# Value weights that arrive already transposed: eight transposing loads in place of TensorE's turns, with a rewritten TensorE order

## The chip, the core and the metric

The kernel runs on one core of a Trainium2 chip. The core has five engines with a queue of instructions each: TensorE (PE: matmuls, with its weight loads shown as PEld), VectorE (DVE), ScalarE (ACT), GpSimd (POOL) and SyncE (SP). SP computes nothing here; it issues nearly all DMAs. The engines meet only through semaphores. On-chip data lies in SBUF (128 partitions); TensorE writes its results to PSUM, eight banks of 128 x 512 floats, and DVE or ACT must copy ("evict") them to SBUF before a bank is free again. The metric is device time in microseconds (us), the median of several runs of the whole program.

## The reference, cut to what matters

Two layers are applied to 2048 tokens of width 448, and each layer is an attention with a carried memory followed by a gated MLP. Attention goes over 64 segments of 32 tokens; each segment sees 8 memory rows besides its own tokens, and its own output at these 8 rows is the next segment's memory, so the segments form a chain.

```python
for s in range(n_seg):                                  # 64 segments, in order
    h = concat([mem, x[s]])                             # 8 + 32 rows of width 448
    q, k, v = h @ Wq, h @ Wk, h @ Wv                    # 16 heads of 256
    p = softmax(mask(q @ k.T * scale))
    o = einsum('bhte,hed->btd', p @ v, Wo)
    mem = o[:, :8]; outs.append(o[:, 8:])
...
x = x + A(layernorm(x)); x = x + B(layernorm(x))        # B: relu(x Wg) * (x Wu) @ Wd
x = x + A(layernorm(x)); x = x + B(layernorm(x))        # the same weights again
```

## The kernel before, in words

**Folded weights.** The kernel multiplies the weights together once, at the start. For each head it forms A = Wq Wk^T (448 x 448) and B = Wv Wo (448 x 448), and afterwards works on A and B alone: scores are h A h^T, and the output is (p h) B. TensorE contracts over partitions, so the product Wv Wo over the 256 head columns needs Wv with these columns on partitions. In DRAM Wv has its 448 rows first. The turned form is `lhs[e, et, d] = Wv[d, 128 et + e]`.

**The start, in order.** `weights` loads Wq and Wk in four groups (`g`), turns them on TensorE, and multiplies them into A. Then it goes over eight pairs of heads (`p`, 512 columns of Wv each). In the kernel before, a pair has four loads on SP's queue: rows 64 to 447 of Wv (`load`), two pieces with rows 0 to 63 (one for each head), and 448 KB of Wo. `transposes` (line 842, its last turn line 843) then turns each head with seven 128 x 128 matmuls against an identity into one PSUM bank. Two copies by DVE or ACT (line 399 is the ACT form, line 402 the DVE form) bring it to the `WT` buffers in SBUF. `product` (line 860) makes six products of 128 rows and one of the 64-row tails for a pair, each into a PSUM bank that is then copied into `Bsb`, the SBUF home of B.

**Buffers.** `Bsb` is also the staging area of Wq and Wk (slots 0 to 11), so a value product can be stored there only when the staged Wq and Wk of that place have been turned. A pair's Wv goes to slot `12 + p % 5`, its Wo to slot `p % 5`: pairs 5, 6 and 7 take over the slots of pairs 0, 1 and 2. Slots 12 to 14 lie in `glu` (the later home of the MLP weights), 15 and 16 in the two `Ug` buffers; the Wo slots lie in `glu`, `YT` and `hG`. The identity, the mask, and zeroed buffers are made by `constants` at the very start, together with dummy matmuls on zeros (line 303) that keep TensorE busy while the first weights arrive.

**After the start.** `chain` is one step of the memory recurrence (71 steps, the second layer seven segments behind the first): its matmuls with A (line 1029), the softmax in `middle` (lines 1186 to 1275), the matmuls with B (line 1066). `tiles` adds the attention of whole tiles of 128 tokens (lines 1356 to 1431) and the MLP (lines 1453 and 1471). `norm` prepares a tile (its turn is line 1304). `glu_part` issues the loads of the MLP weights (line 947) as steps complete.

**What sets the order.** A planner (`_Sched`) places every operation with estimated costs and writes one instruction list for each engine with the semaphore waits. TensorE's list isn't chosen by it: `ORDER` is a written permutation of all TensorE operations, and each waits in that order until its inputs and its banks are ready. A late operation holds up everything behind it on TensorE. For the other engines the planner takes whichever ready operation has the best priority. `turn` in `schedule` reads `ORDER`; `alias` entries tell which buffers share a place; `room` makes an operation wait for what its destination's next writer would have to wait for. The planner charges a DMA its bytes at 300 bytes per ns (`DMA_RATE`) and SP 620 ns for each issue (`DMA_ISSUE`).

Of the kernel before, what the change touches and what calls it, by code (L numbers as in the profile page):

```python
# [12 lines left out]
D = 448  # L13
# [392 lines left out]
def bass_interleave_layers__memory_aug_recurrent_mem_tr__glu_gated_reglu__prompt_kernel(  # L406
# [22 lines left out]
    0, 4, 1, 6, 5, 7, 15, 16, 30, 11, 14, 10, 9, 13, 18, 17, 2, 8, 12, 24, 23, 19, 20, 22, 25, 21, 27, 29, 39, 28,  # L429
    3, 26, 40, 38, 41, 35, 33, 34, 31, 47, 46, 32, 48, 37, 36, 44, 42, 45, 43, 62, 49, 50, 51, 52, 60, 61, 63, 54, 59, 53,  # L430
    57, 55, 66, 68, 67, 69, 56, 58, 64, 70, 65, 74, 72, 73, 71, 82, 83, 85, 84, 79, 80, 75, 76, 78, 91, 77, 81, 90, 89, 87,
    86, 88, 92, 111, 121, 112, 103, 102, 120, 118, 115, 94, 106, 125, 122, 104, 123, 105, 113, 93, 108, 127, 114, 124, 126, 109, 167, 168, 119, 128,
    110, 101, 169, 170, 116, 157, 165, 171, 107, 138, 98, 117, 173, 95, 147, 96, 97, 148, 156, 100, 172, 99, 129, 130, 149, 139, 154, 133, 174, 150,
    132, 161, 160, 151, 131, 140, 142, 163, 145, 136, 158, 137, 155, 146, 164, 159, 152, 144, 141, 134, 162, 143, 153, 175, 135, 176, 227, 177, 178, 228,
    229, 179, 180, 230, 184, 185, 182, 183, 181, 187, 186, 188, 231, 189, 232, 233, 241, 190, 242, 191, 243, 192, 193, 194, 244, 195, 199, 197, 200, 198,
    196, 202, 201, 203, 204, 245, 246, 247, 205, 255, 206, 256, 207, 208, 257, 166, 209, 210, 258, 212, 214, 213, 215, 211, 234, 216, 218, 217, 259, 219,
    260, 261, 269, 270, 220, 235, 248, 221, 236, 271, 272, 273, 274, 275, 237, 222, 223, 249, 238, 239, 224, 225, 262, 250, 295, 296, 293, 294, 226, 251,
    276, 298, 297, 299, 263, 240, 252, 264, 265, 300, 253, 254, 277, 301, 266, 302, 278, 279, 303, 304, 267, 268, 280, 305, 281, 306, 282, 308, 310, 309,
    311, 307, 283, 358, 284, 313, 312, 314, 285, 315, 359, 286, 316, 317, 287, 318, 319, 320, 288, 321, 323, 324, 325, 326, 322, 327, 328, 329, 289, 330,
    290, 292, 331, 291, 332, 368, 333, 334, 335, 338, 336, 337, 367, 360, 339, 341, 342, 340, 377, 344, 361, 345, 343, 352, 369, 346, 353, 385, 354, 347,  # L440
    362, 376, 363, 348, 386, 349, 350, 364, 370, 378, 351, 371, 372, 406, 404, 405, 407, 355, 365, 418, 410, 408, 409, 420, 366, 411, 373, 379, 356, 419,
    374, 421, 412, 357, 380, 413, 387, 381, 414, 415, 416, 375, 388, 382, 383, 422, 417, 389, 390, 426, 427, 424, 425, 429, 384, 428, 430, 391, 431, 392,
    393, 432, 439, 438, 440, 486, 423, 433, 494, 434, 394, 441, 435, 436, 395, 396, 437, 442, 446, 444, 447, 445, 443, 449, 459, 448, 450, 460, 458, 451,
    399, 400, 461, 452, 398, 453, 495, 454, 455, 456, 397, 485, 457, 462, 401, 402, 467, 468, 465, 466, 487, 470, 464, 469, 471, 496, 480, 403, 479, 472,
    503, 463, 473, 504, 474, 512, 481, 488, 475, 476, 477, 489, 490, 513, 497, 482, 505, 491, 498, 478, 492, 531, 533, 534, 532, 499, 506, 514, 537, 545,
    536, 546, 535, 493, 538, 483, 500, 484, 508, 507, 539, 501, 540, 622, 541, 542, 543, 547, 502, 509, 515, 510, 548, 544, 517, 516, 551, 552, 553, 554,
    511, 555, 557, 556, 549, 518, 558, 519, 520, 559, 566, 621, 550, 613, 560, 530, 567, 565, 521, 561, 562, 563, 522, 523, 564, 568, 573, 574, 571, 572,
    576, 526, 575, 577, 586, 585, 569, 578, 524, 579, 570, 580, 525, 581, 582, 583, 587, 612, 527, 588, 584, 528, 529, 614, 630, 631, 589, 623, 591, 639,
    590, 615, 594, 595, 592, 593, 617, 616, 640, 597, 596, 598, 606, 618, 619, 599, 620, 607, 608, 641, 624, 632, 600, 649, 601, 650, 626, 625, 602, 603,
    604, 633, 627, 651, 635, 675, 634, 605, 628, 694, 695, 696, 697, 629, 642, 609, 698, 700, 699, 643, 644, 666, 667, 701, 636, 637, 610, 652, 709, 702,  # L450
    668, 703, 611, 685, 704, 705, 706, 710, 708, 638, 645, 711, 646, 707, 647, 716, 714, 717, 715, 654, 653, 676, 729, 648, 655, 669, 712, 720, 719, 730,
    718, 656, 677, 721, 684, 713, 722, 659, 723, 776, 671, 724, 725, 726, 661, 670, 658, 660, 728, 727, 662, 734, 735, 736, 737, 657, 731, 738, 740, 686,
    739, 678, 749, 672, 741, 748, 750, 663, 664, 732, 742, 665, 743, 733, 785, 679, 744, 745, 746, 784, 680, 775, 693, 747, 751, 754, 757, 758, 755, 756,
    673, 759, 760, 769, 761, 674, 762, 681, 687, 771, 752, 786, 777, 763, 770, 753, 688, 764, 682, 765, 766, 767, 802, 794, 803, 768, 689, 832, 833, 830,
    831, 772, 778, 683, 835, 836, 834, 845, 844, 846, 690, 804, 837, 691, 773, 692, 847, 838, 780, 774, 839, 793, 779, 840, 841, 842, 787, 781, 789, 788,
    921, 782, 843, 795, 848, 850, 852, 851, 853, 783, 854, 796, 866, 856, 855, 790, 857, 797, 798, 791, 805, 858, 792, 849, 859, 807, 799, 806, 860, 861,
    862, 800, 864, 801, 865, 808, 863, 812, 867, 872, 870, 873, 871, 809, 875, 876, 874, 884, 885, 810, 877, 868, 911, 912, 869, 878, 811, 920, 879, 815,
    880, 881, 882, 813, 814, 816, 883, 817, 818, 819, 886, 922, 820, 913, 938, 930, 824, 939, 887, 890, 914, 822, 929, 821, 915, 916, 823, 893, 894, 891,
    892, 888, 825, 897, 896, 895, 826, 905, 898, 923, 827, 940, 906, 828, 931, 899, 889, 924, 900, 975, 901, 902, 903, 949, 925, 974, 950, 907, 904, 917,
    932, 1004, 1002, 1003, 1005, 908, 918, 1007, 1006, 1008, 829, 919, 934, 933, 926, 927, 941, 1009, 928, 935, 1018, 1016, 976, 1010, 909, 951, 1011, 910, 983, 943,  # L460
    942, 1012, 1013, 1014, 984, 992, 1017, 952, 936, 1015, 1019, 985, 1022, 1024, 1025, 1023, 1020, 937, 1027, 1038, 1026, 1028, 1037, 944, 1036, 1029, 945, 946, 1030, 953,
    1021, 993, 1031, 1083, 1032, 1033, 1034, 947, 1039, 1084, 954, 958, 959, 961, 960, 977, 1035, 962, 1042, 1044, 1045, 1043, 955, 1058, 1046, 1047, 1040, 1048, 1057, 963,
    948, 1049, 964, 956, 1050, 1056, 965, 1051, 1041, 969, 967, 979, 1052, 1053, 1054, 966, 978, 968, 1055, 986, 1059, 957, 980, 1062, 1065, 1066, 1063, 1064, 1068, 1060,
    1078, 994, 1069, 1079, 1067, 1085, 1077, 970, 1070, 971, 1080, 972, 1071, 973, 1061, 1072, 1093, 988, 987, 1073, 1074, 1075, 1081, 995, 1092, 1082, 981, 1076, 982, 1138,
    1140, 1141, 1139, 997, 996, 989, 1144, 1143, 1001, 1142, 990, 1145, 1152, 991, 1153, 1154, 1086, 1094, 1146, 1102, 1147, 1111, 1148, 1149, 1150, 1101, 1087, 1110, 1088, 1151,
    1103, 1095, 1160, 1158, 1161, 1159, 1155, 998, 1162, 1174, 1164, 1163, 1172, 1089, 1165, 999, 1000, 1090, 1166, 1156, 1112, 1167, 1157, 1220, 1096, 1097, 1168, 1169, 1170, 1104,
    1091, 1173, 1098, 1099, 1171, 1175, 1105, 1106, 1178, 1179, 1180, 1181, 1100, 1176, 1183, 1182, 1113, 1192, 1184, 1193, 1194, 1107, 1185, 1108, 1115, 1114, 1177, 1186, 1109, 1187,
    1228, 1188, 1189, 1190, 1116, 1120, 1117, 1118, 1195, 1191, 1219, 1229, 1221, 1119, 1237, 1238, 1121, 1122, 1123, 1124, 1125, 1196, 1126, 1230, 1239, 1222, 1127, 1128, 1130, 1223,
    1246, 1247, 1131, 1224, 1258, 1198, 1231, 1225, 1248, 1226, 1199, 1201, 1202, 1200, 1197, 1129, 1232, 1132, 1257, 1233, 1133, 1205, 1204, 1203, 1214, 1240, 1134, 1206, 1135, 1227,
    1234, 1215, 1136, 1207, 1259, 1235, 1242, 1208, 1241, 1236, 1249, 1209, 1210, 1211, 1251, 1283, 1250, 1282, 1243, 1213, 1212, 1244, 1312, 1310, 1311, 1313, 1137, 1245, 1216, 1316,  # L470
    1314, 1315, 1325, 1324, 1284, 1260, 1317, 1252, 1253, 1318, 1254, 1217, 1319, 1291, 1301, 1218, 1292, 1326, 1255, 1320, 1321, 1322, 1261, 1266, 1262, 1267, 1269, 1327, 1323, 1293,
    1332, 1330, 1333, 1331, 1263, 1336, 1256, 1334, 1335, 1345, 1328, 1346, 1264, 1337, 1270, 1271, 1285, 1344, 1338, 1265, 1339, 1329, 1275, 1287, 1340, 1341, 1342, 1286, 1268, 1274,
# [1126 lines left out]
```

## Time and profile before

| what | value |
|---|---|
| median of 3 runs | 1540.95 us (1539.51 to 1541.03) |
| profiled execution: its own time | 1542.45 us |
| profiled execution: span from first to last instruction | 1540.7 us |
| mean granted TensorE clock | 0.998 of full speed |
| instructions | 85641 |
| ScalarE busy | 870.4 us (56%) |
| GpSimd busy | 61.7 us (4%) |
| bytes moved by DMA | 34.20 MB, mean 22 GB/s |
| TensorE turns Wq and Wk, makes A | 6.8 to 44.7 us |
| TensorE turns Wv, makes B | 44.7 to 77.1 us |

The page splits the span into 40 slices of 38.5 us; the start that the change touches is the first two of them. Busy time of TensorE is modelled as if each matmul occupied it from start to end, so that matmuls that overlap are counted once. A line of the groups gives the engine, the source line, the operands by the program's names, the number of instructions, the busy time, and the mean duration of one. An idle time is followed by an arrow and what ended it. In the list of windows, the number after each engine is its busy time in that stretch, and x is the count of instructions.

### The profile page before, as it was taken

To read this page: it belongs to the slowest core of one execution; us is meant where nothing else is said; L and a number is where in the kernel's file an instruction comes from. 1 tells how busy PE (TensorE), PEld (TensorE's weight loads), DVE (VectorE), ACT (ScalarE), POOL (GpSimd) and SP (SyncE) were. 2 spreads that over 40 slices of the span, in tenths; PEclk is the share of its full clock that TensorE was granted. 3 is DMA by queue.
4 is the path that set the end of the run, shared out by engine and by line. 5 is a ranking of instruction groups with operands and counts; after the bars stand their busy time and mean duration, and the time that the engine had idled before them with its cause. 6 is when DMAs were issued, how large, how long until landed. Compare 5 with 4: busy or idle time off the path is not lost.

```text
span 1540.7 us, 85641 instructions
## 1 busy us (share of the span) xinstructions
PE 1525.0 (99%) x38921; PEld 1116.2 (72%) x38921; DVE 1154.1 (75%) x3388; ACT 870.4 (56%) x2434; POOL 61.7 (4%) x254
## 2 busy tenths in 40 slices
PE   9989999999999999999999999999999999999999
PEld 7567767677768777777768776777768776677676
DVE  7736678877877778768876878687877778677675
ACT  6844556555665655555654556455655556455543
POOL 1000000000000000000000000000000000000000
PEclk9999999999999999999999999999999999999999
DMA  8531000000000000000000000000000000000000
GB/s 244 159 88 49 10 8 12 8 9 8 8 5 14 8 8 14 5 15 6 17 5 7 13 9 14 5 15 7 18 5 7 13 5 17 4 9 7 8 11 12
DMA packets 44410, 34.20 MB, mean 22 GB/s; under 512 B 14216, under 2 KB 43152, under 8 KB 44048
## 3 DMA queue, kind: packets, MB, share of 16 engines
q1 hardware_dynamic: 43728, 28.45, 6.8%
q8 instruction: 307, 5.03, 1.3%
q14 instruction: 55, 0.45, 0.1%
q10 hardware_dynamic: 320, 0.26, 0.1%
HBM read 21.35 MB, written 1.84 MB: 15 GB/s over the span
## 4 chain that ended last, share of the span: by engine, by line
PE 94%; DVE 2%; SPq 2%; DMA 1%; issue 1%; ACT 1%; ACTq 0%; DVEq 0%
PE psG L1356 16%; PE psG L1431 16%; PE psC L1066 11%; PE psG L1453 11%; PE psC L1029 9%; PE psG L1471 5%; PE psG L1029 3%; PE psG L1271 3%; PE psG L1384 2%; PE psC L1186 2%; PE psG L1066 2%; PE psG L860 2%; PE psG L1186 2%; SPq L807 1%; PE psC L1209 1%; PE psC L1271 1%
## 5 line engine op out<-in xcount | busy, mean ns | idle before, releaser
L1431 PE MATMUL psG<-Bsb,YT 128*128 128x448 bf16 x1344 | 291.8, 353 | 0.0
L399 ACT ACTIVATE Ug<-psG 64x128 bf16<-64x128 f32 (+2 forms) x437 | 154.4, 368 | 85.0 <-PE psG L1356 67.4
L1431 PEld LDWEIGHTS psG<-Bsb,YT 128*128 128x128 bf16 x1344 | 115.9, 97 | 92.9 <-issue 8.9
L1453 PE MATMUL psG<-G,glu 64*128 64x128 bf16 x5544 | 182.6, 216 | 0.2 <-ACT hG L1458 0.2
L1453 PEld LDWEIGHTS psG<-G,glu 64*128 64x128 bf16 x5544 | 169.6, 94 | 7.6 <-issue 5.2
L1066 PE MATMUL psC<-Bsb,YTm 128*32 128x448 bf16 (+2 forms) x3752 | 171.8, 336 | 0.2 <-ACT YTm L399 0.2
L1356 PE MATMUL psG<-HT,A 64*128 64x128 bf16 x3256 | 171.1, 216 | 0.2 <-ACT Bsb L399 0.2
L1029 PE MATMUL psG<-A,mT 64*32 64x448 bf16 x4004 | 165.4, 350 | 0.5 <-DVE mT L402 0.2
L1029 PE MATMUL psC<-A,mT 64*32 64x448 bf16 x3836 | 162.2, 350 | 2.3 <-issue 1.7
L1356 PE MATMUL psG<-HX,A 64*128 64x128 bf16 x2442 | 146.0, 216 | 0.0
L1066 PEld LDWEIGHTS psC<-Bsb,YTm 128*32 128x32 bf16 x3752 | 94.1, 98 | 57.5 <-DVE YTm L402 0.7
L1029 PEld LDWEIGHTS psC<-A,mT 64*32 64x32 bf16 x3836 | 81.8, 92 | 58.0 <-ACT mT L399 3.7
L402 DVE CAST YT<-psG 128x448 bf16<-128x448 f32 x164 | 99.2, 617 | 27.2 <-PE psG L1275 26.4
L1356 PEld LDWEIGHTS psG<-HT,A 64*128 64x128 bf16 x3256 | 113.4, 94 | 7.6 <-issue 4.0
L399 ACT ACTIVATE YT<-psG 128x448 bf16<-128x448 f32 x205 | 104.5, 542 | 24.0 <-PE psG L1275 21.7
L402 DVE CAST Ug<-psG 64x128 bf16<-64x128 f32 (+2 forms) x245 | 105.0, 437 | 17.3 <-PE psG L1356 13.5
L1458 ACT ACTIVATE hG<-psG 128x512 bf16<-128x512 f32 (+1 forms) x121 | 65.9, 545 | 88.4 <-PE psG L1453 81.8
L1083 DVE TENSOR_TENSOR Osum<-psC,Osum 32x448 f32<-32x448 f32 (+2 forms) x110 | 67.0, 609 | 55.1 <-ACT Osum L1081 52.6
L1471 PE MATMUL psG<-glu,hG 128*128 128x448 bf16 x448 | 100.9, 353 | 0.0
L1029 PEld LDWEIGHTS psG<-A,mT 64*32 64x32 bf16 x4004 | 84.6, 92 | 18.2 <-issue 3.1
L1356 PE MATMUL psG<-l,A 64*128 64x128 bf16 x2821 | 96.7, 216 | 0.0
L1356 PEld LDWEIGHTS psG<-HX,A 64*128 64x128 bf16 x2442 | 92.4, 94 | 0.0
(295 smaller groups left out, 3126.8 us busy)
## 6 DMA issues: line engine op xcount, KB each, us to landing
Bsb<-in_A_Wq_dram SPq DMA_DIRECT2D x6, 384.0 KB
Bsb<-in_A_Wk_dram SPq DMA_DIRECT2D x6, 384.0 KB
glu<-in_A_Wv_dram SPq DMA_DIRECT2D x6, 384.0 KB
Tsb<-Ohi SPq DMA_DIRECT2D x128, 7.0 KB
X<-in_A_x_dram SPq DMA_DIRECT2D x16, 112.0 KB
glu<-in_A_Wo_dram SPq DMA_DIRECT2D x4, 448.0 KB
out_dram<-X SPq DMA_DIRECT2D x16, 112.0 KB
glu<-in_B_W_gate_dram SPq DMA_DIRECT2D x7, 224.0 KB
```

Of the source, the lines that this page charges most:

```text
L399: return E.activation(out, i, ACT.Copy, scale=1.0 if scale is None else scale)
L402: return E.tensor_copy(out, i)
L1029: i = E.matmul(ub[v].ap()[32 * j:32 * j + 32, 0:D], lhsT=self.mT[rw, b, :], rhs=self.A[rw, b, a0:a0 + D], start=(b == 0), stop=(b == 6), t ...
L1066: x = E.matmul(bo.ap()[32 * j:32 * j + 32, 0:d1 - d0], lhsT=self.YTm[:, q, :], rhs=self.Bsb[:, chunks[q], d0:d1], start=(i == 0), stop=(i ...
L1083: s.add("dve", dv_cost(n), lambda E, e, j=j, a_=a_, part=part: E.tensor_tensor(a_, part(j), a_, ALU.add), r=[bo], w=w, part=(j, 0), **P)
L1186: i = E.matmul(view()[:, :, k, v], lhsT=self.Usb[:, o:o + 128], rhs=Sel[:, :].rearrange("p (c q) -> p c q", c=2), start=True, stop=True)
L1271: return E.matmul(ps[:, n * q:n * q + n], lhsT=HR[rows, KM + 128 * q:KM + 128 * q + 128], rhs=PT, start=True, stop=True, tile_position=(b, 0))
L1356: i = E.matmul(ub[v].ap()[:, 128 * n:128 * n + 128], lhsT=self.A[rw, b, a0:a0 + 128], rhs=HT[rw, b, :, 0:SEG] if b < 4 else HX[rw, b - 4, ...
L1431: i = E.matmul(bo.ap()[:, 0:D], lhsT=YT[:, c, :], rhs=self.Bsb[:, 14 * g + c, :], start=(g == 0 and c == 0), stop=(g == 3 and c == 13))
L1453: i_ = E.matmul(two[v].ap()[:, 128 * c:128 * c + 128], lhsT=self.Wgu[rw, b, f0:f0 + 128], rhs=G[rw, b, :], start=(b == 0), stop=(b == 6), ...
L1458: s.add("act", 169 + 0.84 * N, lambda E, e, dst=dst, z=two[0], N=N: E.activation(dst, z.ap()[:, 0:N], ACT.Relu), r=[two[0]], w=[("hG", i, ...
L1471: i_ = E.matmul(bk.ap()[:, 0:D], lhsT=hG[:, c, :], rhs=self.Wd[:, c, :], start=(c == 0), stop=(c == NFC - 1))
```

## The change

A pair's Wv no longer comes by three loads and two sets of turns. One DMA (`turn_dma`, issued by SP with the transposing flag) reads the 448 x 512 block of Wv and writes it turned, as `V[e, a, d]` with 128 partitions and four blocks of 448, into the first 1792 columns of the same slot `12 + p % 5`. `product` reads its stationary operand straight from that slot. The eight pairs lose 24 loads, 112 turning matmuls and 32 copies, and get 8 transposing loads. The planner charges such a load 150000 bytes more than it carries.

A slot is now read by the pair's products, not by its turns, so the load of pair 5 waits for the products of pair 0 (and 6 for 1, 7 for 2). `product` gets `room=w`: it may not be placed before the operations that still use the place in `Bsb` to which its result goes. TensorE has 2711 operations in place of 2727, and its whole written order is another one, from the first entry to the last; the numbering shifts by up to 16 because of the removed operations.

```diff
 ORDER = (
-    0, 4, 1, 6, 5, 7, 15, 16, 30, 11, 14, 10, 9, 13, 18, 17, 2, 8, 12, 24, 23, 19, 20, 22, 25, 21, 27, 29, 39, 28,
...
+    4, 7, 0, 5, 6, 15, 1, 16, 2, 3, 30, 17, 18, 8, 11, 10, 14, 13, 21, 24, 12, 20, 25, 9, 23, 22, 19, 26, 39, 27,
...
 )
...
+    def turn_dma(self, dst, src, nbytes, r=(), w=(), prio=None):
+        self.s.add("sp", 60, lambda E, e: E.dma_start(dst, src, transpose=True), r=r, w=w, dma=nbytes + self.TURN_EXTRA, prio=prio)
+
+    TURN_EXTRA = 150000
...
-            s.add("pe", mm_cost(D, D), fn, r=[k for q in terms for k in q[5]], w=[bk], alloc=[bk], mode=mode, prio=0)
+            s.add("pe", mm_cost(D, D), fn, r=[k for q in terms for k in q[5]], w=[bk], alloc=[bk], room=w, mode=mode, prio=0)
...
         for p in range(NPAIR):
             sv = 12 + p % 5
             so = p % 5
-            load(self.Wv_d, p, sv)
-            for hh in range(2):
-                c = 512 * p + 256 * hh
-                self.dma(self.Wst[sv][64 * hh:64 * hh + 64, 3, 0:256], self.Wv_d[0:64, c:c + 256], 32768, w=[("Wt", sv, hh)])
+            V = self.Wst[sv].rearrange("p a b -> p (a b)")[:, 0:4 * D].rearrange("p (a b) -> p a b", a=4)
+            self.turn_dma(V, self.Wv_d[:, 512 * p:512 * p + 512], 458752, w=[(z, sv) for z in ("Wst", "Wst3")])
             self.dma(self.Wos[so][:, :, :], self.Wo_d[:, 4 * p:4 * p + 4, :], 458752, w=[("Wos", so)])
-            tv = nw()
-            transposes([(sv, hh) for hh in range(2)], tv, True, self.Wst[sv][:, 3, 0:256], [("Wt", sv, hh) for hh in range(2)])
             tails = []
             for hh in range(2):
-                r = tkeys(tv + hh) + [("Wos", so)]
-                rhs = self.Wos[so][:, 2 * hh:2 * hh + 2, :]
+                r = [("Wst", sv), ("Wos", so)]
+                lhs, rhs = V[:, 2 * hh:2 * hh + 2, :], self.Wos[so][:, 2 * hh:2 * hh + 2, :]
                 for k in range(3):
-                    product(self.Bsb[:, b_idx(k, p, hh), :], [(self.WT[tv + hh], 64 + 128 * k, 128, rhs, 0, r)], [("B", p, hh, k)], 0)
-                tails.append((self.WT[tv + hh], 0, 64, rhs, 64 * hh, r))
+                    product(self.Bsb[:, b_idx(k, p, hh), :], [(lhs, 64 + 128 * k, 128, rhs, 0, r)], [("B", p, hh, k)], 0)
+                tails.append((lhs, 0, 64, rhs, 64 * hh, r))
             product(self.Bsb[:, b_tail(p), :], tails, [("B", p, hh, 3) for hh in range(2)], 3)
```

In the new order, two products of pair 0 stand among the last products of A, and the first product of pair 4 stands ahead of the first of pair 3.

## The prediction

> **What bounds the kernel now.** I read the page's busy shares first, then its 40 slices.
>
> ```profile
> PE 1525.0 (99%) x38921; PEld 1116.2 (72%) x38921; DVE 1154.1 (75%) x3388; ACT 870.4 (56%) x2434; POOL 61.7 (4%) x254
> ...
> PE   9989999999999999999999999999999999999999
> ...
> DMA  8531000000000000000000000000000000000000
> ```
>
> TensorE has work in 99% of the span, and DMAs matter only in the first slices. So what is taken from TensorE shortens the run only if TensorE is also unbroken where the change sits. The busy time by stage (boundaries where turns of Wv start and products of B end) shows that:
>
> ```profile
> 36.00:44.70 8.70, 8.70 (x114) 6.21 (x112) 7.36 (x18) 7.11 (x14) 0.00 (x0) 1.00 1.08 345
> 44.70:77.10 32.40, 31.92 (x378) 19.23 (x376) 23.18 (x55) 27.60 (x60) 1.05 (x2) 1.00 0.42 124
> 77.10:150.00 72.90, 67.78 (x1880) 49.25 (x1880) 37.07 (x111) 33.14 (x96) 2.96 (x12) 0.98 0.28 72
> 150.00:300.00 150.00, 147.46 (x4041) 108.28 (x4047) 114.49 (x344) 84.91 (x247) 6.39 (x28) 1.00 0.04 10
> 300.00:1450.00 1150.00, 1148.85 (x30080) 845.16 (x30065) 887.79 (x2633) 655.43 (x1872) 43.31 (x184) 1.00 0.04 10
> ```
>
> Columns: stretch, length, busy time of PE, PEld, DVE, ACT and POOL, granted clock, DMA share, GB/s. In the B stage TensorE lacks 0.48 us of 32.40, DVE and ACT have room, and DMAs are at 42%. From 300 to 1450 us TensorE lacks 1.15 us. A saving made in the B stage is therefore not swallowed later. The waits of TensorE from 12 to 77 us are one line, a Wv load; the timeline beside it shows what a turn costs:
>
> ```profile
> PE psG L842 <- DMA Ug<-in_A_Wv_dram: 0.5, 1, 0.5
> ```
>
> ```profile
> 46.15 0.50 PE L842 MATMUL psG<-ident,glu 128*128 128x128 bf16 x6
> 46.48 0.22 PE L843 MATMUL psG<-ident,glu 128*128 128x128 bf16 x1
> 46.54 0.50 PE L842 MATMUL psG<-ident,glu 128*128 128x128 bf16 x6
> 46.87 0.22 PE L843 MATMUL psG<-ident,glu 128*128 128x128 bf16 x1
> 46.93 0.50 PE L842 MATMUL psG<-ident,glu 128*128 128x128 bf16 x6
> ```
>
> The seven turns of a head start 0.39 us after those of the one before (46.15, 46.54, 46.93): they overlap, and 0.39 us is what a set takes from TensorE. Last, SP's issues, and how the DMAs do on small packets (answer for 200 to 400 us):
>
> ```profile
> L807 SPq DMA_DIRECT2D glu<-in_A_Wv_dram x18: 376/586/1205, 31.3 to 54.2; - x18
> L807 SPq DMA_DIRECT2D Ug<-in_A_Wv_dram x6: 497/552/1587, 39.0 to 43.6; - x6
> L807 SPq DMA_DIRECT2D glu<-in_A_Wo_dram x4: 368/486/594, 33.7 to 65.0; - x4
> ```
>
> ```profile
> q1 hardware_dynamic: 3309, 1.07, 2.4%
> ```
>
> The first Wv is issued at 31.3 us, right after the last piece of Wk.
>
> **The change part by part.** *Turns removed.* 16 sets x 0.39 = 6.24 us of TensorE, on the path, since nothing else holds TensorE in this stage. The wait of 0.48 us at 45.3 goes if the first loads are early. As a check I walked both written orders with durations from the timeline (0.39 a set of turns, 0.392 a product of A, 0.379 a product of B, 0.73 a part of the memory's first product, 0.25 a norm's turn, 0.3 others), set so that the third group's products end where the trace has them. The old walk ends B at 76.9 us (trace 77.1), the new one at 70.6.
>
> The Trainium skill, TensorE: Matmul & The Clock Gate, Part 4, gives 275 ns for a turn in a kernel and says that turns don't raise the clock. By it 112 turns would be an estimated 30.8 us. The trace disagrees: 0.39 / 7 = 56 ns each, at a granted clock of 1.00 from 36 to 44.7 us, and 6.24 stands.
>
> *Copies removed.* 16 wide and 16 narrow, 13.0 us of DVE and ACT together in the group rows (ACT 6.8, DVE 6.2). Off the path: 0. What remains is 56 copies of 0.54 to 0.62 us, some 16 us an engine, in a stage of 26 us.
>
> *24 loads removed, 8 added.* SP issues two DMAs for a pair instead of four, 0.59 us each: 9.4 us less on its queue. Behind Wv and Wo stand only the loads of x for tiles 2 and 3, the memory rows and tile 1's rows, which are used after 100 us. If a transposing issue took the longest that a row of SP shows (1.8 us, a load of rows by line 807), five pairs would take 12 us in place of 13.6. Cost 0.
>
> *Time of a transposing load, T.* The trace has none. Nearest row for the bytes: 35 to 45 us at 338 GB/s, which makes 458752 B 1.36 us. Nearest row for small packets: 2.4% x 16 x 200 us / 3309 = 23.2 ns each. A source row of 512 columns falls into four pieces of 256 B, since each block has 128 partitions: 1792 pieces on 16 engines, 2.6 us. At the far end, single elements of 2 B would make 333 us a load. I take 2.0, between the first two, because whole pieces of rows are read as in the plain loads; the planner's own charge, 608752 B at 300 per ns, is 2.03.
>
> When does T reach the path? In the new walk the pairs' first products stand at 39.2 (0), 46.2 (1), 48.5 (2), 52.6 (4), 53.3 (3), 57.7 (5), 62.1 (6) and 65.8 us (7). Bytes flow from 32.6 us (1 us after the first issue, as for the isolated Wo at 60.5), and each pair takes T + 1.36. Pair 4 is fifth in the queue: 32.6 + 5 x (T + 1.36) <= 52.6 gives T <= 2.6, the tightest. Pairs 5 to 7 wait for the last products of pairs 0 to 2 (51.8, 55.2, 59.9 us); with 1 us to the first byte they allow T up to 3.5, 4.5 and 3.5. So all of 1.36 to 2.6 is hidden: cost 0. If that cover is gone, each us above 2.6 costs 5 us at pair 4, and above 3.5 another 2 at pairs 5 and 7. The gain is used up near T = 3.8 us.
>
> By the Trainium skill, DMA: Bandwidth & Descriptors, Latency and other measured facts, a transposing DMA with a broken middle dimension does 261 GB/s, an estimated 1.76 us here, which would also be hidden. No run so far shows one.
>
> *`room` in `product`.* The operations that it adds are turns on TensorE itself, earlier in its list; the loads they read have been awaited by them. No wait: 0. Had it one, all of TensorE's list would stand behind it.
>
> *The rest of the order.* In the first 12 us the new order puts all turns of the first group ahead of its first product. They need 1.84 MB; 0.78 + 1.40 MB have moved by 10 us. 0. After B, the order can win at most the idle of 77 to 150 us (5.1) and of 150 to 300 us (2.5); what it can lose isn't shown by any row. From 300 to 1450 us there is nothing to win. I take 0, with +4 and -11 as bounds of the gain: most of the first stretch, and the loss in the last rival.
>
> *Sum.* 6.24 + 0.48 = 6.72 us. The profiled execution takes 1542.45 (span 1540.7, 1.75 around it), so 1535.73; it is 1.5 us above the median 1540.95, which goes to **1534.2**.
>
> **The rivals.** *Loads partly late (T 2.6 to 3.8).* For: the transposing pattern is new, and pair 4's 2.6 us is just the small-packet price. Against: up to there the queue is covered. At T = 3.2 it loses 3.0 at pair 4: 1537.2.
>
> *Loads late, slower than before.* Place: pair 4's first product, held on TensorE with all behind it, from T = 3.8 on. For: pieces of 256 B might be charged 23.2 ns both read and written, T = 5.2. Then 13.0 at pair 4 and 3.4 at pairs 5 and 7 make 16.4 - 6.7 = 9.7 us slower: 1550.6. Against: the plain loads read and write in one pass.
>
> *Loads far slower, down to 2-byte pieces.* This is also the case that the load isn't done as one transposing transfer. At T = 20 us pair 4 alone is 87 us late: above 1620; at 333 us it is milliseconds. The Trainium skill, VectorE: DVE Perf Modes, The three transpose paths, has 1309 ns for one 128 x 128 block by DMA; 14 blocks one after another would be an estimated 18.3 us a load and some 1640 in all. No row of the trace speaks for blocks done singly.
>
> *The rest of the order is worse.* TensorE stops for 1.2 to 1.8 us at "issue" in two of the first steps (1.8 at line 1271, 1.7 in two at line 1029). With such a stop in four more of the 71 steps the gain is gone; with six, 10.8 - 6.7 = 4.1 slower: 1545. Against: from 300 us on such stops are missing.
>
> **How the numbers follow.** About 0.2%, 3 us, is what a measurement of this kernel can tell from no change. Forecast 0.62 (its own range 1530 to 1537.5: the rest of the order at +4 and at -3); partly late 0.13 (faster 0.04, same 0.07, slower 0.02); late 0.13 and far slower 0.04, all slower; order worse 0.08 (same 0.02, slower 0.06). Faster 0.66, same 0.09, slower 0.25. Below 1530 I leave 0.05. To leave no more than 0.15 above, the range must take in most of the late case: it ends at 1550, leaving out the far case and those above T = 5.
>
> **What would show it.** Right: no lines 842 and 843 on Wv, about 112 matmuls and 32 copies fewer, the last product of B near 70.5 us, no wait of TensorE for Wv, and about the same idle after it. The DMA part should show one transposing issue a pair, 1.4 to 2.6 us of DMA time each. Wrong: TensorE waiting at a product for Wv, first at pair 4; DMAs near 100% from 33 to 65 us with few GB/s; an SP issue of over 3 us; or B's end at 70.5 us and the gain missing at 150 us or later, which would be the order.

## The result and the profile after

The changed kernel takes 1560.2 us (median of 4 runs, 1560.1 to 1561.87); the kernel before, 1540.23 (4 runs, 1537.76 to 1541.03). The ratio is 1.0139, 95% interval 1.0126 to 1.0152: 20 us slower, where 6.7 us faster was forecast. The profiled execution takes 1560.1 us, with a span of 1558.3.

The first readings are the page's busy shares, slices and packets of the changed kernel:

```profile
PE 1536.6 (99%) x38904; PEld 1117.7 (72%) x38904; DVE 1139.7 (73%) x3315; ACT 877.6 (56%) x2486; POOL 58.7 (4%) x243
...
DMA  9631000000000000000000000000000000000000
...
DMA packets 54521, 34.19 MB, mean 22 GB/s; under 512 B 28424, under 2 KB 53264, under 8 KB 54160
```

TensorE is busy for 99% of a span that is 17.6 us longer, so the busy share alone shows no fault. Packets under 512 B were 14216 before: 14208 more, against 8 x 1792 = 14336 pieces of 256 B. The loads do run in such pieces. Matmuls fell by only 17, not by 112, and the lines of line 303 (dummy matmuls on zeros) say why:

```profile
L303 PE MATMUL psC<-warm x73: 219/314/314, 1.0 to 7.7; 128*128 128x128 bf16 x73
L303 PE MATMUL psG<-warm x75: 216/219/220, 311.9 to 1515.2; 128*128 128x128 bf16 x75
```

Columns are ns (min, median, max), then first and last start in us. Before had 53 of the first kind and none of the second. The 75 stand deep in the memory steps; 20 + 75 more dummies and 112 fewer turns are the 17.

Busy time by stage of the changed kernel, in the columns of the table of before:

```profile
44.70:77.10 32.40, 26.37 (x252) 12.53 (x251) 18.21 (x37) 17.68 (x39) 1.05 (x3) 0.89 0.61 152
150.00:300.00 150.00, 147.69 (x4036) 107.12 (x4030) 112.70 (x346) 82.83 (x246) 6.39 (x28) 1.00 0.04 10
300.00:1450.00 1150.00, 1145.63 (x29631) 838.97 (x29617) 862.35 (x2524) 660.85 (x1905) 39.35 (x169) 1.00 0.04 10
```

Two losses show. In the B stage TensorE lacks 6.03 us where it lacked 0.48, and the granted clock is 0.89 instead of 1.00. From 300 to 1450 us it lacks 4.37 where it lacked 1.15, and it gets through 449 matmuls fewer in the same 1150 us (29631 against 30080, dummies included) while it looks 99.6% busy.

To split the two, take the start of the last matmul of a value product (line 860 before, 865 after) as the end of the start. It is at 76.8 us before and 77.2 after. What follows lasts 1463.9 us before and 1481.1 after. **So the start came out even (+0.4), and the rest lost 17.2 us.** Two things failed, not one.

In the start, TensorE's waits in the changed kernel were (line waited at, releaser, us, times, longest):

```profile
PE psG L865 <- DMA glu<-in_A_Wo_dram: 4.2, 1, 4.2
PE psG L865 <- DMA hG<-in_A_Wo_dram: 1.8, 1, 1.8
```

`hG` holds pair 4's Wo, the first `glu` slot pair 5's. SP's timeline of the changed kernel (start us, duration us) shows what was ahead of them:

```profile
33.22 3.42 SPq L807 DMA_TRANSPOSE glu<-in_A_Wv_dram  x1
...
44.98 2.81 SPq L807 DMA_TRANSPOSE Ug<-in_A_Wv_dram  x1
47.83 0.58 SPq L812 DMA_DIRECT2D hG<-in_A_Wo_dram  x1
48.45 0.98 SPq L812 DMA_DIRECT2D X<-in_A_x_dram  x2
49.47 1.74 SPq L812 DMA_DIRECT2D HR<-in_A_mem_dram  x2
51.26 5.00 SPq L812 DMA_DIRECT2D HR<-xn  x8
56.30 1.55 SPq L807 DMA_TRANSPOSE glu<-in_A_Wv_dram  x1
57.90 0.59 SPq L812 DMA_DIRECT2D glu<-in_A_Wo_dram  x1
```

In this trace a transposing issue holds SP for 1.49 us where no other value load is under way (pair 7, at 66.76) and up to 3.42 us while the DMAs are full; the plain ones of Wo between them, of the same size, take 0.57 to 0.59. And tile 1's eight row loads stand ahead of pair 5's Wv: it is issued at 56.30, though its slot is free some five us earlier. TensorE asks for that pair at 58.06 and gets it at 62.27. The windows of the changed kernel behind that wait show a second price:

```profile
60.00:65.00 5.00, 2.73 (x11) 1.44 (x12) 0.62 (x1) 0.84 (x2) 0.00 (x0) 0.53 1.05 267
65.00:70.00 5.00, 5.00 (x33) 2.17 (x32) 3.27 (x8) 3.59 (x10) 0.24 (x1) 0.78 0.41 93
```

The granted clock falls to 0.53 and 0.78: some 2.4 us lost by (1 - 0.53) x 2.73 + (1 - 0.78) x 5.00, an estimate. In full, it stood at 0.50 from 60.3 to 67.1 us. The Trainium skill, TensorE: Matmul & The Clock Gate, Part 1: The HAM clock gate, says that TensorE goes to half rate once idle for a window of about 3.4 us; the trace agrees in the rate, 0.50, but not in the length. The clock fell 2.2 us into the stop of 4.2 us, and in a kernel further down (tile 1's rows last, second execution) a stop of 2.4 us was followed by 0.50 from 54.3 to 57.7 us.

### The profile page after: what moved, and what is told of

It is laid out like the page before. It is cut to its first block, busy times and chain, and to the rows that moved or that the text cites. A ratio compares the mean times of both kernels' runs of the same rounds, so it can differ in the third digit from the quotient of the medians.

```text
span 1558.3 us, 85547 instructions
## 1 busy us (share of the span) xinstructions
PE 1536.6 (99%) x38904; PEld 1117.7 (72%) x38904; DVE 1139.7 (73%) x3315; ACT 877.6 (56%) x2486; POOL 58.7 (4%) x243
## 4 chain that ended last, share of the span: by engine, by line
PE 91%; DVE 4%; SPq 3%; DMA 1%; issue 1%; ACT 1%; POOL 0%; DVEq 0%; POOLq 0%
PE psG L1432 16%; PE psG L1357 16%; PE psC L1067 11%; PE psG L1454 11%; PE psC L1030 8%; PE psG L1472 5%; PE psG L1030 4%; PE psG L1272 3%; PE psG L1385 2%; PE psC L1187 2%; PE psG L1187 1%; PE psC L1210 1%; SPq L812 1%; PE psG L1067 1%; PE psG L865 1%; PE psC L1272 1%
## 5 line engine op out<-in xcount | busy, mean ns | idle before, releaser
L399 ACT ACTIVATE Ug<-psG 64x128 bf16<-64x128 f32 (+2 forms) x428 | 150.1, 367 | 86.6 <-PE psG L1357 73.9
L1454 PE MATMUL psG<-G,glu 64*128 64x128 bf16 x5684 | 187.0, 216 | 0.1
L1067 PE MATMUL psC<-Bsb,YTm 128*32 128x448 bf16 (+2 forms) x3920 | 180.0, 335 | 0.2 <-issue 0.2
L1030 PE MATMUL psG<-A,mT 64*32 64x448 bf16 x4060 | 154.6, 350 | 2.8 <-issue 2.4
L1030 PE MATMUL psC<-A,mT 64*32 64x448 bf16 x3780 | 148.8, 350 | 0.7 <-issue 0.4
L402 DVE CAST Ug<-psG 128x256 bf16<-128x256 f32 (+2 forms) x247 | 105.7, 436 | 21.7 <-PE psG L1357 17.8
L1084 DVE TENSOR_TENSOR Osum<-psC,Osum 32x448 f32<-32x448 f32 (+2 forms) x118 | 71.9, 609 | 64.1 <-ACT Osum L1082 61.4
L1030 PEld LDWEIGHTS psC<-A,mT 64*32 64x32 bf16 x3780 | 74.6, 92 | 52.8 <-ACT mT L399 4.9
L1030 PEld LDWEIGHTS psG<-A,mT 64*32 64x32 bf16 x4060 | 78.3, 92 | 25.5 <-issue 4.1
L1357 PE MATMUL psG<-l,A 64*128 64x128 bf16 x2842 | 91.1, 216 | 0.0
```

What stands on the lines that cost most here:

```text
L399: return E.activation(out, i, ACT.Copy, scale=1.0 if scale is None else scale)
L402: return E.tensor_copy(out, i)
L1030: i = E.matmul(ub[v].ap()[32 * j:32 * j + 32, 0:D], lhsT=self.mT[rw, b, :], rhs=self.A[rw, b, a0:a0 + D], start=(b == 0), stop=(b == 6), t ...
L1067: x = E.matmul(bo.ap()[32 * j:32 * j + 32, 0:d1 - d0], lhsT=self.YTm[:, q, :], rhs=self.Bsb[:, chunks[q], d0:d1], start=(i == 0), stop=(i ...
L1084: s.add("dve", dv_cost(n), lambda E, e, j=j, a_=a_, part=part: E.tensor_tensor(a_, part(j), a_, ALU.add), r=[bo], w=w, part=(j, 0), **P)
L1357: i = E.matmul(ub[v].ap()[:, 128 * n:128 * n + 128], lhsT=self.A[rw, b, a0:a0 + 128], rhs=HT[rw, b, :, 0:SEG] if b < 4 else HX[rw, b - 4, ...
```

## The experiments

Theory A: the loss is the new written order's own, behind the value products. Theory B: it comes from the transposing loads and what they hold up. Both can be true at different places; the runs put a size on each. This table has the profiled execution of each kernel, in us: end of the start as above, span, and the difference, "rest". The kernels ran on three chips, on which the kernel before took 1541.45 (new start, tile 1's rows last, old order, new order in before), 1539.64 (the same once more, plain loads, the 80 changes of shape) and 1538.05 us (the last three experiments), so a rest is best compared within one of these groups.

| kernel | start's end | rest | span |
|---|---|---|---|
| before | 76.8 | 1463.9 | 1540.7 |
| changed | 77.2 | 1481.1 | 1558.3 |
| new start, old rest | 79.9 | 1464.5 | 1544.4 |
| ... tile 1's rows last | 72.2 | 1468.4 | 1540.6 |
| ... the same once more | 74.3 | 1464.6 | 1538.9 |
| ... plain loads | 69.1 | 1465.7 | 1534.8 |
| ... both tiles' rows late | 73.0 | 1461.8 | 1534.8 |
| ... and start reordered | 70.0 | 1461.5 | 1531.5 |
| changed, old order | 81.2 | 1466.8 | 1548.0 |
| before, new order | 83.9 | 1480.5 | 1564.4 |
| before, rows last | 74.3 | 1462.7 | 1537.0 |

### The new order's start with the old order's rest

```diff
 ORDER = (
-    (all of the new order)
+    (the new order up to the last value product, then what is left of the old one, less 16 for the removed turns)
```

> The changed kernel, with the new order only up to the last product of B and the old order (renumbered) for all that comes after. Theory A: the loss of 18 to 20 us is made after 77 us, by the new order of the rest (the first memory steps to the end take 1480.8 us in place of 1463.6), and the start alone comes out even, because late loads give back the 6 us of the turns. Then this kernel runs 1538 to 1544 us. Theory B: the transposing loads are to blame, for the whole run: 1555 to 1562 us, as changed.

Measured: 1544.53 us (1540.29 to 1547.21), before 1541.45; ratio 1.0019 (1.0007 to 1.0031). That is half a us above the range of theory A. The rest is back at 1464.5, with every transposing load in place. So the 17 us are the order behind the value products. What stays is the start, which ended 2.7 us later than in the changed kernel this time: its waits were 3.4 us for pair 4 and 2.8 us for pair 5.

### The old order throughout

```diff
-ORDER = (new)
+ORDER = (old, without the turns of Wv, less 16)
-... alloc=[bk], room=w, mode=mode ...
+... alloc=[bk], mode=mode ...
```

> The changed loads with the old written order throughout (turns dropped, renumbered; the extra wait of the products on their destination's users is left out, which the old order doesn't allow). Theory A: the rest takes what it took before, and the start, which asks for pairs 2, 3, 1 and 0 at once, waits some us for the fourth pair: 1538 to 1547 us. Theory B: 1555 or more.

Measured: 1549.93 us (1545.59 to 1550.73); ratio 1.0046 (1.0033 to 1.0058). Some 3 us above what the order theory had set, and below what the load theory needed. The rest is 1466.8; the start ends at 81.2, 4.4 later than before, with waits for Wo of 2.3 and 1.6 us at two slots. With these loads the old start is worse than the new one; the old rest is better than the new one.

### The turns and plain loads of before, in the new order

```diff
-ORDER = (old)
+ORDER = (new, with each pair's two sets of turns put in ahead of its first product)
```

> The kernel before (plain loads, turns on TensorE), with the new written order; a pair's turns stand right ahead of its first product, and pair 0's first two products behind the last of A. Theory A: the rest costs its 17 us also without any transposing load, and the start takes the 6 us of the turns and some more, since the order wasn't made for turns: 1557 to 1570 us. Theory B: 1538 to 1546 us.

Measured: 1566.83 us (two runs, 1566.23 and 1567.42); ratio 1.0161 (1.0137 to 1.0186). There is no transposing load in this kernel, and its rest is 1480.5: the same 17 us. Its start ends at 83.9; the order of the start was not made for the turns that were put in. For the rest, theory A is settled from both sides.

### What in the new order costs: 80 more changes of tile shape

A matmul's form in the trace gives the part of the array that it uses: 128\*128, 64\*128, 128\*32. Counted along the traces behind 77.5 us (40\*128 counts as 64\*128), neighbouring matmuls differ in that form 572 times before and 648 times after; 573 with the new start and old rest. To price one such change alone, 40 pairs of neighbouring operations were swapped in the kernel before, between 300 and 1400 us, so that a run of one shape is broken by another.

```diff
 ORDER = (
-    ..., a, b, ...
+    ..., b, a, ...        (40 places, each adding two changes of shape)
```

> The kernel before, with 40 pairs of neighbours in TensorE's written order exchanged between 300 and 1400 us, each at a border of two groups of different tile shapes, so that TensorE changes its tile shape 80 times more (the changed kernel's order has 78 more than before). Nothing else is changed, and no exchange crosses a dependency. Theory A: part of the 17 us that the new rest costs is such changes, at 40 to 95 ns each: 3 to 8 us slower. Rival: a change of shape hides under the matmuls already running, then it is within 1.5 us of before, and the whole loss is in waits.

Measured: 1550.46 us (1547.53 to 1555.22), before 1539.64; ratio 1.0066 (1.005 to 1.0082): 10.8 us for 80 changes, 0.135 us each (0.10 to 0.16 by the interval). That is more than expected. TensorE's busy share shows nothing of it; this is the long window of that kernel:

```profile
300.00:1450.00 1150.00, 1148.09 (x29780) 837.82 (x29777) 878.70 (x2591) 652.37 (x1863) 42.91 (x182) 1.00 0.04 10
```

TensorE lacks 1.91 us of 1150, yet finishes 300 matmuls fewer than before did (30080). The Trainium skill, TensorEngine Tiling (Array Packing), Tiling Modes, Key Properties, says that changing the tiling mode drains TensorE; it gives no price. The run agrees, with 0.135 us each.

The other part is visible in TensorE's timeline of the changed kernel (start, us, line, matmuls; in brackets the idle time before and its releaser):

```profile
311.67 0.37 PE L1210 MATMUL psC<-l,uTr 128*128 128x40 bf16 x8
311.88 1.44 PE L303 MATMUL psG<-warm 128*128 128x128 bf16 x23
313.50 0.26 PE L1109 MATMUL psG<-Sel,Ohi 128*128 128x16 bf16 x4 [0.18 <-POOL Ohi L967]
313.62 1.00 PE L303 MATMUL psG<-warm 128*128 128x128 bf16 x15
```

Here the new order leaves TensorE nothing to do until a chain over POOL and DVE is through, and the kernel's builder fills such a planned stop with dummies on zeros. They stand at 311.9 (38), 818.0 (7), 1178.6 (11) and 1514.2 (19): 75 at 56 ns are 4.2 us.

A first account of the 17.2 us, estimated from these rows: 76 changes x 0.135 = 10.3; dummies 4.2; 3.2 more idle from 300 to 1450 us; less 2.4, by which the idle time from 77 to 300 us is smaller (2.92 + 2.31 us, against 5.12 + 2.54 before). That is 15.3.

The starts of the matmuls in the traces give a second account, without the price from the swaps. Take the time from each matmul's start to the start of the next, less the median of that time for matmuls of the same form behind which the shape stays. Behind the value products this excess, summed over the changes of shape, is 87.3 us in the trace of before (573 changes, 0.152 us each) and 95.4 us in the changed kernel (649): 8.1 us more. The 75 dummies take 5.7 us from start to start, idle time is 0.7 us more, and 2.7 us are left without a name; together 17.2. The kernel with the old loads and the new order gives the same 8.1 and 5.7. In the kernel with the 40 swaps the same sum is 13.0 us above before, so its added time does stand at the changes of shape.

Both accounts give the changes of shape 8 to 10 us and the dummies 4 to 6. Neither was removed by itself from the new rest: their shares are worked out, not shown, and 2 to 3 us stay open.

### Tile 1's rows behind the value loads

```diff
-def dma(self, dst, src, nbytes, r=(), w=(), prio=None):
+def dma(self, dst, src, nbytes, r=(), w=(), prio=None, after=()):
...
+late = self.v_last if (t, l) == (1, 0) else ()
-self.dma(..., w=[("HRx", l, b, p, h)], prio=prio)
+self.dma(..., w=[("HRx", l, b, p, h)], prio=prio, after=late)
```

(on the new start with the old rest; `v_last` holds the last pair's two loads)

> As e3, and the eight small DMAs of tile 1's rows (5 us of SP) are issued behind the last Wv and Wo loads instead of ahead of pair 5's. Theory A: in the changed kernel SP reached pair 5's load at 56.3 us only because of them; without them at about 51, so TensorE's wait of 4.2 us for pair 5 goes, and with it most of the low clock (0.53 and 0.78 from 60 to 70 us). 3 to 6 us below e3: 1533 to 1539 us. Rival C: pairs 5 to 7 are held by the time of the transposing loads themselves (3.8 us for a pair of Wv and Wo), so the wait only moves: within 1.5 us of e3.

Measured: 1540.77 us (1537.76 to 1544.04), before 1541.45; ratio 0.9996 (0.9984 to 1.0008). That is 3.8 us below the kernel beside it, as theory A had it, and 1.8 us above its range. SP's timeline of this kernel:

```profile
50.77 0.67 SPq L812 DMA_DIRECT2D HR<-in_A_mem_dram  x2
51.48 2.63 SPq L807 DMA_TRANSPOSE glu<-in_A_Wv_dram  x1
...
67.56 5.00 SPq L812 DMA_DIRECT2D HR<-xn  x8
```

and its waits for loads of a value product:

```profile
PE psG L865 <- DMA hG<-in_A_Wo_dram: 2.4, 1, 2.4
```

Pair 5's load goes out at 51.48 instead of 59.05 and its wait is gone; the start ends at 72.2, not 79.9. Pair 4's wait remains. So the rows on SP's queue made the wait at pair 5. Of the 7.7 us only 3.8 reached the end of the run: the rest is 1468.4, 4 us longer than in the kernel beside it. Two of its windows in the first memory steps:

```profile
93.40:96.80 3.40, 3.38 (x80) 1.65 (x88) 0.00 (x0) 0.00 (x0) 0.00 (x0) 0.50 0.02 5
103.60:107.00 3.40, 3.27 (x65) 2.82 (x69) 0.00 (x0) 0.31 (x2) 0.00 (x0) 0.51 0.85 209
```

The clock stands at half speed in both, which costs some 1.7 us each (an estimate, half of 3.4). A second time the same kernel (below) had a clock of 1.00 in both stretches and a rest of 1464.6. So nearly all of this give-back goes with the clock, and it differs from execution to execution.

### The same kernel beside one with plain loads

To price the turning in the DMA alone, the kernel above ran again beside one whose eight value loads are plain: in place of Wv they bring the same number of bytes of the pair's Wo block, in its own layout, to the same place. That kernel multiplies Wo by Wo, so B is not the reference's; all else is computed as before.

```diff
-E.dma_start(dst, src, transpose=True)
+E.dma_start(dst, src)
...
-self.turn_dma(V, self.Wv_d[:, 512 * p:512 * p + 512], 458752, ...)
+self.turn_dma(V, self.Wo_d[:, 4 * p:4 * p + 4, :], 458752, ...)
```

> The same kernel as e4 with tile 1's rows last, on the chip and beside the kernel before of this group, as the measure for the plain loads: 1537 to 1544 us.

> As e4, but the eight loads into the value slots are plain: they bring the pair's Wo block, in its own layout, in place of the turned Wv block, so the same bytes arrive and nothing is turned (left out: the products multiply Wo by Wo). It prices the turning in the DMA. Theory A: SP's issue falls from 2.2 to 3.9 us to 0.6, a pair's two loads take 2.8 us of DMA time in place of 3.8, TensorE's wait for pair 4 (2.4 us) and the idle of 50 to 55 us are gone, and B ends at 69 to 70.5 us in place of 72.2: 1536 to 1540 us in all, 1 to 4 below e4 on the same chip. Rival: the copies of B's products or the memory's first step hold the start, then B's end stays at 72 us and the time within 1 us of e4.

Measured, before at 1539.64: transposing 1539.11 us (1536.85 to 1541.63), ratio 0.999 (0.998 to 1.0001); plain 1536.8 us (1533.49 to 1538.46), ratio 0.9976 (0.9965 to 0.9988). The transposing form of the loads costs 2.3 us of the run, and 5.2 us at the start's end (74.3 against 69.1). The window from 50 to 55 us, first of the transposing kernel:

```profile
50.00:55.00 5.00, 2.58 (x13) 1.07 (x12) 1.95 (x4) 1.62 (x4) 0.00 (x0) 0.93 1.07 235
```

then of the plain one:

```profile
50.00:55.00 5.00, 5.00 (x34) 2.34 (x32) 4.37 (x9) 3.99 (x9) 0.00 (x0) 1.00 0.54 175
```

With plain loads TensorE runs through and the DMAs are half idle. SP has issued the loads of the first five pairs at 41.5 us, against 49.5 with transposing ones. A plain issue isn't always short: those of line 807 take 0.37 to 2.19 us in this kernel, the longest while the DMAs are full:

```profile
30.65 0.59 SPq L807 DMA_DIRECT2D glu<-in_A_Wo_dram  x1
33.12 2.19 SPq L807 DMA_DIRECT2D glu<-in_A_Wo_dram  x1
```

The start is 7.7 us shorter than before's: this is what the removed turns are worth where no load is late. The run is shorter by 2.8 us only.

### Both tiles' rows behind the values

```diff
-late = self.v_last if (t, l) == (1, 0) else ()
+late, rows = (self.v_last if (t, l) == (1, 0) else ()), (2 if t == 0 else prio)
-self.dma(..., prio=prio, after=late)
+self.dma(..., prio=rows, after=late)
```

> As e4 (new order for the start, old order for the rest, tile 1's rows last), and tile 0's eight row DMAs, which hold SP for 5 to 6 us around 20 to 25 us while DMAs idle, are issued behind pair 4's Wo instead of ahead of the last Wk loads. Theory A: the value loads follow one another at 3.8 us a pair, so all five start 5 us earlier, pair 4 has landed before TensorE asks for it at 50 us, its wait of 2.4 us goes and the clock stays at 1.00: B ends at 69 to 71 us, 2 to 5 us below the kernel before: 1535 to 1538 us. Rival C: pairs 5 to 7, whose slots come free only after pairs 0 to 2, then hold TensorE in its place: B's end at 72 to 74 us, and the time that of before.

Measured: 1536.51 us (1532.94 to 1539.49), before 1538.05; ratio 0.999 (0.9981 to 0.9998). Tile 0's rows, which the changed kernel issues at 19.5 us among the last loads of Wq and Wk, now follow pair 4's Wo, and the first value load goes out at 23.62 instead of 30.32; SP's timeline of this kernel:

```profile
23.62 4.58 SPq L807 DMA_TRANSPOSE glu<-in_A_Wv_dram  x1
...
43.82 0.58 SPq L812 DMA_DIRECT2D hG<-in_A_Wo_dram  x1
...
46.18 5.53 SPq L812 DMA_DIRECT2D HR<-xn  x8
51.75 1.55 SPq L807 DMA_TRANSPOSE glu<-in_A_Wv_dram  x1
53.34 0.59 SPq L812 DMA_DIRECT2D glu<-in_A_Wo_dram  x1
```

and its wait at a value product:

```profile
PE psG L865 <- DMA glu<-in_A_Wo_dram: 2.9, 1, 2.9
```

Pair 4's Wo is issued 4 us earlier than in the changed kernel and its wait is gone, but the eight rows now stand ahead of the loads of pairs 5 and 6, and a new wait of 2.9 us stands at pair 5: its Wo, issued at 53.34, lands at 58.4, and TensorE goes on at 58.5. The time is in the range of theory A; the start's end, 73.0, is that of rival C. Rows that are moved come to stand in front of something else.

### A start ordered for the measured issue

The kernel above, with three edits:

```diff
-free[e] = t0 + self.DMA_ISSUE
+free[e] = t0 + (2900.0 if o.dma == 458752 + 273000 else self.DMA_ISSUE)
-TURN_EXTRA = 150000
+TURN_EXTRA = 273000
 ORDER = (small moves, most of them among the first 330 entries; after them nearly all of the old order)
```

> As the kernel with both tiles' rows behind the value loads, with the planner told what the traces show of a transposing load (2.9 us of SP and 2.44 us of DMA in place of 0.62 and 2.03) and the written order changed by small moves, mostly in the first 330 entries, to suit it. Theory A: about the same as that kernel, within 3 us, since what is left to win in the start is 1 to 2 us: 1533 to 1539 us. Rival: the small moves cost shape changes later, over 3 us slower than it.

Measured: 1533.74 us (1530.87 to 1534.76), before 1538.05; ratio 0.9973 (0.9962 to 0.9983). The planner charges 2.9 us for a transposing issue, a middle value of the traces, and the start was ordered to that. The waits at value products shrink to one:

```profile
PE psG L865 <- DMA glu<-in_A_Wo_dram: 1.4, 1, 1.4
```

The start ends at 70.0 us, near the 70.6 of the walk, 3.0 us earlier than in the kernel above, with the same rest (1461.5 against 1461.8). The kernel is 4.3 us faster than before: faster than both kernels of this case. The loads in the changed kernel were right; the order around them was not.

### The control: rows last in the kernel before

The two edits on the rows, in the kernel before.

> The kernel before (plain loads, turns on TensorE, old order), with both tiles' row DMAs issued behind the value loads as in the two kernels beside it: the control for the move of the rows. Theory A: the start of the kernel before is held by TensorE, which waited for a load for 0.48 us only, so the move gives 0 to 1 us: 1538 to 1542 us. Rival: the rows' place alone makes the gain, then this kernel is as fast as the two others.

Measured: 1538.12 us (1535.41 to 1539.22), before 1538.05; ratio 1.0 (0.9991 to 1.0008). The rows' place by itself is worth nothing in the run, and the 4.3 us are not from it. The start ends at 74.3 us in this kernel, 2.4 us earlier than in the trace of before; there is no trace of the kernel before on this chip to tell whether the rows did that.

## Why the prediction was wrong, point by point

**The rest of the order: the step that failed.** It was taken at 0, and measured +17.2 us. The rival "the rest of the order is worse" had the side and the place right at a chance of 0.08, but another mechanism and too small a price, 10.8 us at six stops: it asked for stops at "issue" in the memory steps, while the runs point to changes of tile shape, which no idle row shows, and to planned stops filled with dummies. The step's reason was that "what it can lose isn't shown by any row", and that does not hold. The two written orders were in the diff, each operation's shape is known from the kernel, and 648 against 572 changes is a count. The planner in the kernel charges a change of shape 95 ns (`TURN`), which makes 76 of them 7.2 us. And the starts of the matmuls in the trace of before show 0.152 us a change. "From 300 to 1450 us there is nothing to win" was read from idle time alone, and falls with it: 410 changes of shape stand in that stretch of before, and hardly any of their time shows as idle. A whole new order of 2711 operations was treated as if it could hardly lose.

**SP's cost at 0: wrong.** The transposing issue was taken at 1.8 us at most; it takes 1.5 to 3.4. And "Behind Wv and Wo stand only the loads of x for tiles 2 and 3, the memory rows and tile 1's rows" was false: tile 1's eight rows went out at 51.26 to 56.30, ahead of pair 5 (in the trace of before two of them, at 50.41, already stand ahead of a Wv load). The sign "an SP issue of over 3 us" came true. From 33 to 48.5 us the DMAs are full, so the long issues there may be no more than the DMAs' pace, seen from SP; no run tells the two apart.

**T: inside its bounds, above the 2.0 taken.** SP issues pairs 1 to 4 from 33.22 to 48.41, 3.8 us a pair; less 1.36 for Wo, that is an estimated 2.44 us, inside 1.36 to 2.6 and near the end reckoned from small packets: from 33 to 48.5 us the pieces of 256 B took 23.5 ns each, against the 23.2 used. 458752 B in 2.44 us are 188 GB/s, less than the 261 of the Trainium skill, DMA: Bandwidth & Descriptors, Latency and other measured facts. Blocks done singly (18.3 us a load) are ruled out. By the sum with the measured T, pair 4 would have had its loads at 32.6 + 5 x 3.8 = 51.6, in time for 52.6. TensorE asked at 51.0 and the load landed at 52.8: both ends of the sum were off, by 1.6 and 1.2 us, and together they make the 1.8 us there. The margin of 1.0 us was less than the walk could promise.

**Turns and copies removed: right, and lost again.** With loads on time the start ended at 69.1 us (plain loads), against 70.6 in the walk and 76.8 before. In the changed kernel 4.2 + 1.8 us of waits and about 2.4 of lowered clock put it to 77.2: 69.1 + 8.4 = 77.5. So the 6.24 us were taken and given back in the same stage.

**"A saving made in the B stage is therefore not swallowed later": half right.** With plain loads 7.7 us at the start's end became 2.8 us of the run, and 5.9 between the two profiled executions. So 1.8 us were lost behind the start (a rest of 1465.7 against 1463.9); both executions have one piece of 3.4 us at 0.50 there, so the clock isn't it. The other 3 us are the yardstick: before's trace comes from an execution of 1542.45 us, 2.8 us above its median beside the plain loads. Beside the control, which is as fast as before on the same chip, the two kernels run with it keep what their starts gain: 74.3 to 73.0 and to 70.0 us at the start's end are 1.3 and 4.3 us, and the runs are 1.6 and 4.4 us shorter. How the 1.8 us are lost stays open.

**`room`: right.** No wait of TensorE at a value product is for it.

## What to carry to other kernels

A rewritten order is a change of its own, and the largest one here: run the new start with the old rest, and the old with the new, before anything is put down to the edit beside it. Count what an order does to neighbours (changes of tile shape, planned stops), because a busy share of 99% shows neither; the starts of the matmuls and the rows of the dummies do. When a DMA becomes slower to issue, look at everything that stands behind it on its queue, and order for the issue time that the trace shows.

## What the runs showed of the hardware

- A transposing DMA of 448 x 512 bf16 held the issuing queue for 1.49 us with no other value load under way and mostly for 2.6 to 3.9 us with the DMAs full (4.58 and 5.00 right behind the last loads of Wk). The plain DMAs of the same bytes between them took 0.57 to 0.59; where all value loads were plain, 0.37 to 2.19.
- A change of tile shape between neighbouring matmuls cost TensorE 0.135 us (0.10 to 0.16) by the run with 80 more of them, and 0.152 us by the starts of the matmuls in the trace of before; busy time does not show it.
- The granted clock fell to 0.50 in pieces of 3.4 or 6.8 us: from 60.3 to 67.1 us with a stop of 4.2 us that began at 58.06, and from 54.3 to 57.7 behind a stop of 2.4 us. The same kernel had two such pieces in its first memory steps in one execution and none in another, with rests of 1468.4 and 1464.6 us.
